# A written-out instruction order searched anew: weight folding ahead of attention, behind a run of matmuls on zeros

## The chip, the cores and the metric

The kernel runs on one core of a Trainium2 chip. The metric is the device time of one execution in microseconds; below are seven runs of the kernel before the change and one profiled execution. The profile splits an execution into a span (first to last instruction of the program) and what lies around it.

## The reference, cut to what matters

Linear attention with the feature map ELU+1, followed by a feed-forward block whose hidden layer is a product of two projections and has no other nonlinearity:

```python
phi = lambda x: np.where(x > 0, x, np.exp(x) - 1.0) + 1.0
kv  = einsum('bhsd,bhse->bhde', phi(k), v);  z = phi(k).sum(axis=2)
att = einsum('bhsd,bhde->bhse', phi(q), kv) / (einsum('bhsd,bhd->bhs', phi(q), z)[..., None] + 1e-6)
x   = att, heads side by side                   # (4608, 512)
out = ((x @ w1) * (x @ w2)) @ w3 @ w_out        # (4608, 512)
```

There are 8 batches of 8 heads, 576 positions and head width 64. The arrays are float32: q, k, v of 9.4 MB each, w1 and w2 512x1024, w3 1024x1024, w_out 1024x512.

## The kernel before, in words

**Fold.** Nothing stands between w3 and w_out, so the kernel multiplies them once into `wf_sb` (1024x512, bf16). Row block i of w3 is loaded with a cast to bf16 (`load_w3`, step E), transposed on TensorE in eight 128x128 pieces (`w3_tr`, step w, L454), copied out of PSUM (L455), and multiplied with w_out in eight matmuls (`wf_mm`, L464; step W for all eight, or U for the first four and W for the last four), then copied to `wf_sb` (L467). Steps C load the two halves of w_out.

**Attention.** Per batch, `load_qkv` brings k (step L), q (M) and v (N): parts 0 and 1 are heads 0-3 and 4-7 of positions 0-511, part 2 is both, part 3 the last 64 positions, as two small DMAs. The feature map takes three passes: exp on ScalarE (steps x for k, X for q, L137), minimum with 1 (y, Y, L141) and max(x+1, e) on VectorE (z, Z, L162). v is cast to bf16 with a column of ones (step v, L171/L176). Step K makes k'v (L199, added at L204), T transposes phi(q) by a DMA (L242), A makes the quotient (L265, L271 to L275), and its transpose into `xt` is step P (TensorE, L285) or D (a DMA, L296). Batch 0 goes another way: phi(q) is transposed on TensorE (steps a and, for the copy out, b; L309, L311), c makes k'v, d masks it (L320), e makes numerator and denominator already transposed (L330), f forms the reciprocal on ScalarE as exp(-ln) (L335, L336), g multiplies (L339).

**Feed-forward.** The 4608 tokens are nine chunks of 512. F c.f does eight matmuls of 128x128 by 128x512 (L371), one ScalarE copy (L376) and one VectorE product (L377); there are eight F per chunk, and each pair of them reads one quarter of w1 and w2, loaded by step B (two DMAs with a cast). Steps h and i are F0.0 and F0.1, interleaved. O c.m makes one output tile from eight matmuls against `wf_sb` (L390) and copies it (L393); S stores it. Q is the last tile.

**What sets the order.** The kernel is scheduled by hand: `ORDER` is a list of steps, and each engine executes its own instructions in exactly this order. A `+` behind a step chooses the other engine: VectorE instead of ScalarE for a copy, GpSimd's DMA queue instead of SyncE's for a load. `GATES` delays four loads until a named load has landed. Three resources tie steps together. Raw q, k, v and w3 share a rotation of five buffers (pool `ld`; the small parts have eight, pool `ldr`), so a load waits until the buffer's last reader is done: the sixth tile waits for the first one's. PSUM has four `mm` banks, taken in turn by F, O, U/W, P and the first two e, and two double banks `at`, taken by w, a, c, e, K and A. And each queue's DMAs carry eight semaphores in rotation, so a DMA is not issued before the one eight places ahead of it on that queue has landed.

Of the kernel before, what the change touches and what calls it, by code (L numbers as in the profile page):

```python
# [18 lines left out]
def kernel(  # L19
# [59 lines left out]
    vt = wpool.tile([P, NJ, H, D + 1], BF16)  # L79
    vr = wpool.tile([P, H // 2, D + 1], BF16)  # L80

    def constants(part):
        if part == 0:
            make_identity(nc, ident)
        elif part == 1:

# [4 lines left out]
            nc.gpsimd.memset(vt[:, :, :, D:D + 1], 1.0)
            nc.gpsimd.memset(vr[:, :, D:D + 1], 1.0)
        else:
            nc.vector.memset(zero, 0.0)  # L94

# [372 lines left out]


    ORDER = """  # L470
    L0.3 M0.0+ X0.0 L0.0+ I1 Y0.0 x0.2 y0.2 M0.1+ Z0.0 x0.0 Z0.1 y0.0 I2 z0.0 z0.4 L0.1+ N0.3+
    x0.1 H12 N0.0+ N0.1+ X0.1 L1.3+ E0 Y0.1 v0.0 L1.2+ v0.1 z0.1 y0.1 B0 v0.2+ I0 Z0.2 z0.2 Z0.3
    E1 C0 x1.2 a0.0 B1 b0.0 C1 c0.0 M1.3+ z0.3 d0.0 e0.0 a0.1 e0.1 f0.0 f0.1 B2 E2 c0.1 y1.2 E3
    b0.1+ M1.2+ w0 d0.1 g0.0 e0.2 e0.3 f0.2 g0.1 B3 h0.0 f0.3 E4 x1.0 g0.2 z1.4 h0.1 h0.2 g0.3
    h0.3 i0.0 y1.0 i0.1 x1.1 w1 z1.0 F0.2 X1.2 z1.1 N1.3+ y1.1 F0.3 U0 z1.2 W0+ F0.4 E5 M2.3+
    F0.5 Y1.2 X1.0 w2+ E6 Y1.0 Z1.0 N1.0+ w3 W1 W2+ X1.1 F0.6 U3 Z1.1 E7 N1.1+ Y1.1 w4 M2.2+
    Z1.2 W3 v1.0+ a1.0 Z1.3 b1.0 w5 F0.7 X2.2 Y2.2 Z1.4 z1.3 w6 W4 w7 L2.2+ a1.1 v1.1+ b1.1 W5+
    v1.2 K1.0+ L3.3+ K1.1+ L2.3+ W6 X2.0 X2.1 A1.0 Y2.0 Z2.0 x2.0 W7 N2.3+ x2.1 x2.2 A1.1 T1.1
    P1.1 O0.0 O0.1 Y2.1 Z2.4 N2.2+ P1.0 L3.2+ y2.2 y2.0 Z2.1 M0.3+ O0.3 z2.0 y2.1 v2.1 P1.2 Z2.2
    P1.3+ v2.0 z2.1 z2.2 X0.2 Z2.3 Y0.2 z2.4 v2.2+ A1.2 x3.0 T2.0 z2.3 O0.2 M3.3+ S0.3 F1.0 x3.2  # L480
    M3.2+ F1.1 X3.0 Y3.0 K2.0+ y3.0 K2.1+ N3.3 X3.1 F1.2 S0.1 M4.3 F1.3 Z0.4 z3.0 x3.1 y3.2 N3.2
    z3.4 X3.2 F1.4 A2.0 Y3.1 F1.5 M4.2+ T0.1 F1.6 A2.1 P2.1 L4.3 v3.2+ F1.7 Z3.0 Y3.2 D1.1 Z3.1
    S0.0 Z3.2 O1.0 y3.1 P2.2+ X4.2 L4.2 z3.1 r0 Z3.3 v3.1 O1.1+ N4.3 v3.0+ P2.0 X4.0 z3.2 O1.3
    F2.0 T2.1 N5.3 z3.3 T3.0 N4.2+ Z3.4 K3.0+ X4.1 A2.2 Y4.0 Y4.2 F2.1 P2.3 K3.1+ Z4.0 x4.0 y4.0
    F2.2 M5.3 Y4.1 O1.2 z4.0 Z4.4 A3.0 F2.3 L6.3 Z4.1 L5.3 x4.2 Z4.2 F2.4 M5.2 x4.1 P3.0+ S0.2
    T3.1 P3.1 z4.1 Z4.3 F2.5 F2.6 A3.1 X5.0 F2.7 v4.2+ v4.0 y4.1 X5.2 L5.2 P3.2 z4.2 X5.1 S1.0
    O2.2+ S1.1 A3.2 y4.2 P3.3+ T4.0 Y5.0 v4.1 z4.3 x5.0 O2.3+ z4.4 F3.0 F3.1 x5.1 K4.0+ K4.1+
    y5.0 Y5.2 z5.0 Z5.4 S1.3 Z5.0 M6.3 x5.2 T4.1 F3.2 F3.3 Z5.1 D3.1 z5.1 O2.1 Y5.1 A4.0 S1.2
    x6.2 L7.3 Z5.2 F3.4 N5.2 F3.5 S2.3 D2.1 L6.2 v5.1 y5.1 A4.1 z5.2 M6.2+ F3.6 D4.0 y6.2 F3.7
    X6.0 S2.2 z5.3 v5.0+ O2.0 S2.1 O3.0 Z5.3 x6.0 x6.1 O3.2 M7.3 y5.2 T5.0 L7.2 z5.4 Y6.0 O3.3  # L490
    v5.2+ y6.0 F4.0 X6.1 X6.2 K5.0+ Y6.2 K5.1+ F4.1 Y6.1 F4.2 z6.0 F4.3 M7.2 Z6.0 N6.2 A5.0 Z6.4
    F4.4 Z6.1 F4.5 A5.1 Z6.2 O3.1 N6.3 F4.6 T5.1 z6.4 F4.7 y6.1 v6.1 S2.0 D5.0 S3.0 v6.2 z6.1
    z6.2 X7.0 O4.0+ Z6.3 Y7.0 x7.0 y7.0 O4.1+ S3.2 x7.2 T6.0 v6.0 O4.3 A4.2 z6.3 K6.0+ D4.1 F5.0
    F5.1 A5.2 X7.1 K6.1+ F5.2 N7.2+ A6.0 T6.1 S3.3 Z7.0 F5.3 X7.2 F5.4 S3.1 D5.1 Y7.1 F5.5 A6.1
    Z7.1 O4.2+ N7.3 y7.2 v7.0 S4.1 A6.2 F5.6 x7.1 F5.7 Z7.2 y7.1 Z7.3 O5.0+ z7.4 Y7.2 S4.0 D6.0
    S4.3 Z7.4 z7.0 S5.0 O5.1 v7.1 z7.1 O5.2+ F6.0 v7.2 z7.2 T7.1 O5.3 z7.3 K7.0+ K7.1+ F6.1 F6.2
    F6.3 T7.0 S4.2 S5.3 A7.0 F6.4 F6.5 A7.1 F6.6 F6.7 S5.1 D7.0 O6.2+ A7.2 O6.3+ O6.0 F7.0 F7.1
    S6.3 D7.1 S5.2 S6.0 F7.2 F7.3 F7.4 O6.1 F7.5 F7.6 F7.7 D6.1 F8.0 F8.1 S6.1 O7.1 S6.2 F8.2
    F8.3 F8.4 F8.5 O7.3 F8.6 F8.7 S7.3 O7.0+ O8.0+ S7.1 O7.2+ S7.0 O8.1 O8.3 S7.2 S8.1 S8.0 S8.3
    Q8.2  # L500
    """
# [129 lines left out]
```

## Time and profile before

| | us |
|---|---|
| median of 7 runs | 256.8 (256.3 to 260.98) |
| the profiled execution, its own time | 257.56 |
| its span | 255.8 |
| TensorE busy in the span | 235.2 |
| VectorE / ScalarE busy | 167.0 / 130.4 |
| start of the matmuls on zeros / of the first useful matmul (a0.0) | 10.53 / 14.99 |
| start of F1.0 (chunk 1), matmuls | 66.66 |

"Busy" is a union of instruction intervals. A TensorE matmul's record is longer than its place in the pipeline: a 128x512 one is listed with 379 ns, but starts 216 ns after the one ahead. "Idle before" is the time in which the engine had nothing, and the name behind the arrow is what ended it. L numbers are lines of the kernel. Issue and landing times of single DMAs are the trace's events; the page gives medians.

### The profile page before, as it was taken

How to read it: one execution, taken by the hardware profiler on the slowest of the kernel's cores; microseconds unless marked ns; L12 is line 12 of the kernel's file. 1: busy time of each engine (PE TensorE's matmuls, PEld its weight loads, DVE VectorE, ACT ScalarE, POOL GpSimd, SP SyncE). 2: the span in 40 equal slices, each digit the busy share in tenths (PEclk: the TensorE clock that was granted, in tenths of full speed). 3: DMA queues.
4: the chain of work that ended last, by engine and by line, in shares of the span. 5: the costliest groups of instructions: out<-in, count | busy, mean ns of one | idle time of the engine just before them, and what ended most of it. 6: DMA issues, size and time to landing. Idle time of an engine off the chain costs nothing.

```text
span 255.8 us, 4477 instructions
## 1 busy us (share of the span) xinstructions
PE 235.2 (92%) x1641; PEld 114.1 (45%) x1660; DVE 167.0 (65%) x425; ACT 130.4 (51%) x206; POOL 43.1 (17%) x69
## 2 busy tenths in 40 slices
PE   0378999999999999999999999989999999999994
PEld 0144444644454554545445444534454444444442
...
DMA  5999999999999999958968946972470231200225
GB/s 185 363 257 202 211 287 233 320 237 326 271 253 282 269 253 285 272 139 273 325 167 212 367 100 164 259 205 25 143 215 3 55 111 62 82 0 0 83 85 164
DMA packets 58726, 49.52 MB, mean 194 GB/s; under 512 B 34448, under 2 KB 49040, under 8 KB 58704
## 3 DMA queue, kind: packets, MB, share of 16 engines
...
## 4 chain that ended last, share of the span: by engine, by line
PE 74%; DMA 17%; POOL 3%; DVE 3%; issue 1%; ACT 1%; ACTq 0%; SPq 0%; DVEq 0%; POOLq 0%
PE b_ps L371 22%; PE a_ps L371 22%; PE o_ps L390 19%; DMA w_sb<-in_moe_w_dram 4%; PE wf_ps L464 4%; DMA qt<-qj 4%; DMA w3b<-in_moe_w_dram 3%; DMA q32r<-in_q_dram 3%; PE kvp L199 3%; DMA k<-in_k_dram 3%; PE nd L265 2%; PE w3p L454 1%; POOL k L120 1%; PE xtp L285 1%; PE o_ps L417 1%
## 5 line engine op out<-in xcount | busy, mean ns | idle before, releaser
L371 PEld LDWEIGHTS <-w_sb 128*128 128x128 bf16 x576 | 54.4, 98 | 66.5 <-DMA w_sb<-in_moe_w_dram 2.5
L377 DVE TENSOR_TENSOR ab<-a_sb,b_ps 128x512 bf16<-128x512 f32 x72 | 49.2, 685 | 50.9 <-PE b_ps L371 46.5
L371 PE MATMUL b_ps<-xt,w_sb 128*128 128x512 bf16 x288 | 74.9, 379 | 1.1 <-DMA w_sb<-in_moe_w_dram 0.6
L371 PE MATMUL a_ps<-xt,w_sb 128*128 128x512 bf16 x288 | 75.1, 380 | 0.2 <-DMA w_sb<-in_moe_w_dram 0.2
L376 ACT COPY a_sb<-a_ps 128x512 f32<-128x512 f32 x72 | 42.1, 586 | 58.6 <-PE a_ps L371 58.6
L390 PE MATMUL o_ps<-wf_sb,ab 128*128 128x512 bf16 x266 | 63.2, 379 | 1.2 <-ACT wf_sb L467 0.4
L390 PEld LDWEIGHTS <-ab 128*128 128x128 bf16 x280 | 26.8, 98 | 31.5 <-issue 0.7
L393 ACT COPY o_sb<-o_ps 128x512 f32<-128x512 f32 x22 | 12.8, 584 | 38.5 <-PE o_ps L390 38.4
L162 DVE SCALAR_TENSOR_TENSOR qj<-q,e 128x256 bf16<-128x256 f32 x64 | 23.8, 417 | 0.1
L162 DVE SCALAR_TENSOR_TENSOR kj<-k,e 128x256 bf16<-128x256 f32 x64 | 23.7, 415 | 0.0
L141 DVE TENSOR_SCALAR e<-e 128x1024 bf16<-128x1024 bf16 x32 | 13.8, 434 | 12.4 <-ACT e L137 12.4
L137 ACT ACTIVATE e<-q 128x1024 bf16<-128x1024 f32 x16 | 16.9, 1061 | 7.1 <-DMA q<-in_q_dram 7.1
L137 ACT ACTIVATE e<-k 128x1024 bf16<-128x1024 f32 x16 | 16.8, 1056 | 2.9 <-DMA k<-in_k_dram 2.2
L275 DVE TENSOR_TENSOR xn<-nd,r 128x512 bf16<-128x512 f32 x28 | 18.0, 686 | 0.0
L120 POOL DMA_DIRECT2D v<-in_v_dram x7 | 5.9, 850 | 66.8 <-ACT vt L171 44.1
L464 PE MATMUL wf_ps<-wo_sb,w3t 128*128 128x512 bf16 x60 | 14.6, 379 | 0.3 <-issue 0.2
L100 PE MATMUL warm<-zero 128*128 128x512 bf16 x12 | 4.6, 565 | 10.5 <-DVE zero L94 10.5
L171 ACT CAST vt<-v 128x1024 bf16<-128x1024 f32 x12 | 12.6, 1048 | 0.3 <-DMA v<-in_v_dram 0.3
L393 DVE COPY o_sb<-o_ps 128x512 f32<-128x512 f32 x13 | 8.9, 686 | 4.4 <-PE o_ps L390 4.4
L120 POOL DMA_DIRECT2D q<-in_q_dram x7 | 6.1, 876 | 33.3 <-ACT a_sb L376 23.6
L464 PEld LDWEIGHTS <-w3t 128*128 128x128 bf16 x64 | 5.9, 98 | 6.3
L199 PE MATMUL kvp<-vt,kj 64*128 64x130 bf16 x224 | 8.7, 217 | 0.0
...
## 6 DMA issues: line engine op xcount, KB each, us to landing
...
```

The lines of the kernel that those rows point to most:

```text
L120: return (nc.gpsimd if alt else nc.sync).dma_start(out=t[:, h0 * W:h1 * W].rearrange("p (h x) -> p h x", x=W), in_=src[b, h0:h1, 0:NJ * P, ...
L137: nc.scalar.activation(out=e, in_=x, func=AF.Exp)
L141: nc.vector.tensor_scalar_min(out=e, in0=e, scalar1=1.0)
L162: nc.vector.scalar_tensor_tensor(out=out, in0=x, scalar=1.0, in1=e, op0=ALU.add, op1=ALU.max)
L199: nc.tensor.matmul(kvp[:, r, i * W:(i + 1) * W], kk[rows], vv[rows], start=(n == 0), stop=(n == (NJ if r == g else NJ - 1)))
L275: nc.vector.tensor_tensor(out=dst.rearrange("p (c u) e -> p u c e", u=2), in0=v4[:, :, :, 0:D], in1=r[0:n].unsqueeze(3).to_broadcast([n, 2 ...
L371: nc.tensor.matmul(ps, w[:, kc, f * P:(f + 1) * P], xt[:, 4 * c:4 * c + 4, kc, :], start=(kc == 0), stop=(kc == KC - 1))
L376: nc.scalar.copy(out=a_sb, in_=a_ps)
L377: nc.vector.tensor_mul(out=abs_[c][:, f, :], in0=a_sb, in1=b_ps)
L390: nc.tensor.matmul(o_ps, ab[:, f, m * P:(m + 1) * P], wf_sb[:, f, :], start=(f == 0), stop=(f == FC - 1))
L393: copy_of(alt)(out=o_sb, in_=o_ps)
L464: nc.tensor.matmul(wfs[i], w3ts[i][:, kc, :], wo_sb[:, kc, :], start=(kc == 0), stop=(kc == FC - 1))
```

## The change

Three things differ. (1) The constants (mask, eps, the columns of ones) are set by VectorE instead of GpSimd. (2) `ORDER` is a new list. It begins with the identity and the constants; TensorE has 44 matmuls on zeros ahead of everything in place of 12, and then the fold (w, U, W of all eight blocks, every W now split) with batch 0's attention threaded between its second half; w3 and w_out are loaded ahead of v, w1 and w2. Loads of batch 3 and later are all on SyncE's queue (six of them were on GpSimd's). Batch 4's phi(q) is transposed on TensorE (a4.0, a4.1, copied by b4.0, b4.1) in place of the DMA T4.0. Many copies change engines. (3) `GATES` names other loads. Everything else, the helper functions and all tile sizes, is as before, and so is each step's arithmetic.

```diff
-            nc.gpsimd.memset(mask, 0.0)
-            nc.gpsimd.memset(mask[0:D, :, 0, :], 1.0)
-            nc.gpsimd.memset(mask[D:P, :, 1, :], 1.0)
-            nc.gpsimd.memset(eps, 1e-6)
-            nc.gpsimd.memset(vt[:, :, :, D:D + 1], 1.0)
-            nc.gpsimd.memset(vr[:, :, D:D + 1], 1.0)
+            nc.vector.memset(mask, 0.0)
+            nc.vector.memset(mask[0:D, :, 0, :], 1.0)
+            nc.vector.memset(mask[D:P, :, 1, :], 1.0)
+            nc.vector.memset(eps, 1e-6)
+            nc.vector.memset(vt[:, :, :, D:D + 1], 1.0)
+            nc.vector.memset(vr[:, :, D:D + 1], 1.0)
...
-    L0.3 M0.0+ X0.0 L0.0+ I1 Y0.0 x0.2 y0.2 M0.1+ Z0.0 x0.0 Z0.1 y0.0 I2 z0.0 z0.4 L0.1+ N0.3+
-    x0.1 H12 N0.0+ N0.1+ X0.1 L1.3+ E0 Y0.1 v0.0 L1.2+ v0.1 z0.1 y0.1 B0 v0.2+ I0 Z0.2 z0.2 Z0.3
-    E1 C0 x1.2 a0.0 B1 b0.0 C1 c0.0 M1.3+ z0.3 d0.0 e0.0 a0.1 e0.1 f0.0 f0.1 B2 E2 c0.1 y1.2 E3
-    b0.1+ M1.2+ w0 d0.1 g0.0 e0.2 e0.3 f0.2 g0.1 B3 h0.0 f0.3 E4 x1.0 g0.2 z1.4 h0.1 h0.2 g0.3
-    h0.3 i0.0 y1.0 i0.1 x1.1 w1 z1.0 F0.2 X1.2 z1.1 N1.3+ y1.1 F0.3 U0 z1.2 W0+ F0.4 E5 M2.3+
-    F0.5 Y1.2 X1.0 w2+ E6 Y1.0 Z1.0 N1.0+ w3 W1 W2+ X1.1 F0.6 U3 Z1.1 E7 N1.1+ Y1.1 w4 M2.2+
-    Z1.2 W3 v1.0+ a1.0 Z1.3 b1.0 w5 F0.7 X2.2 Y2.2 Z1.4 z1.3 w6 W4 w7 L2.2+ a1.1 v1.1+ b1.1 W5+
-    v1.2 K1.0+ L3.3+ K1.1+ L2.3+ W6 X2.0 X2.1 A1.0 Y2.0 Z2.0 x2.0 W7 N2.3+ x2.1 x2.2 A1.1 T1.1
-    P1.1 O0.0 O0.1 Y2.1 Z2.4 N2.2+ P1.0 L3.2+ y2.2 y2.0 Z2.1 M0.3+ O0.3 z2.0 y2.1 v2.1 P1.2 Z2.2
-    P1.3+ v2.0 z2.1 z2.2 X0.2 Z2.3 Y0.2 z2.4 v2.2+ A1.2 x3.0 T2.0 z2.3 O0.2 M3.3+ S0.3 F1.0 x3.2
...
+    I0 I1 L0.3+ L0.0+ x0.2 M0.0+ I2 x0.0 M0.1 y0.0 X0.0 H6 H11 L0.1+ x0.1 N0.3 E0 E1 X0.1 H3 C0
+    C1 H17 E2 Y0.1 H7 Y0.0 E3 w0 w1+ y0.2 L1.3+ U0 y0.1 Z0.0 E4 z0.0 Z0.1 N0.0+ U1 v0.2 W0 w2 W1
+    Z0.2 M1.3+ w3+ z0.4 U2 z0.1 x1.2 W2 w4+ N0.1+ E5 v0.0 U3 W3 a0.0 E6 b0.0 z0.2 c0.0 z0.3 U4
+    X1.2 v0.1+ E7 d0.0 w5+ M1.2+ c0.1 d0.1 Z0.3 e0.0 f0.0 g0.0 W4+ w6 a0.1 b0.1+ U5 y1.2 e0.1
+    w7+ W5+ X1.0 N1.0+ e0.2 X1.1 Y1.0 Z1.0 Y1.1 L2.3+ B0 v1.0 L1.2+ f0.1 Z1.1 U6 B1 W6+ Y1.2
+    f0.2 B2 U7 M0.3+ W7 e0.3 f0.3 g0.1 z1.4 N1.1+ Z1.2 g0.2 B3 h0.0 g0.3 h0.1 h0.2 Z1.3 x1.0
+    h0.3 a1.0 a1.1 y1.0 i0.0 z1.0 i0.1 Z1.4 x1.1 F0.2 y1.1 z1.1 F0.3 X0.2 b1.1 Y0.2 b1.0+ z1.2
+    z1.3 N1.3 F0.4 v1.2 v1.1 F0.5 L2.2+ Z0.4 K1.0+ K1.1+ x2.2 T0.1 F0.6 M2.3+ A1.0 M2.2 F0.7
+    x2.0 O0.3 N2.2 A1.1 y2.0 P1.1 X2.2 x2.1 T1.1 O0.2+ y2.2 P1.2 X2.0 z2.0 z2.1 N2.3 Y2.0 P1.3+
+    X2.1 z2.4 O0.0+ L3.3 Z2.0 P1.0 v2.0 O0.1+ M3.2 v2.2 x3.2 N3.3 y2.1 Z2.1 L3.2 Y2.2 y3.2 Y2.1
+    F1.0 F1.1 Z2.2 Z2.3 F1.2 z2.2 r0 F1.3 z3.4 z2.3 T2.0 M3.3 K2.0+ F1.4 K2.1+ x3.0 A1.2 X3.1
...
-    z6.2 X7.0 O4.0+ Z6.3 Y7.0 x7.0 y7.0 O4.1+ S3.2 x7.2 T6.0 v6.0 O4.3 A4.2 z6.3 K6.0+ D4.1 F5.0
-    F5.1 A5.2 X7.1 K6.1+ F5.2 N7.2+ A6.0 T6.1 S3.3 Z7.0 F5.3 X7.2 F5.4 S3.1 D5.1 Y7.1 F5.5 A6.1
...
+    x7.2 z6.4 A4.2 A5.2 D5.0 X7.2 T6.1 y7.0 O4.0+ y7.2 Z6.3 O4.3+ K6.0+ T6.0 X7.1 D4.1 z7.4 S4.1
+    K6.1+ F5.0 Y7.2 Z7.4 x7.1 F5.1 F5.2 S4.2 Y7.0 F5.3 v7.2 A6.0 F5.4 F5.5 N7.2 A6.1 z7.0 F5.6
...
-    GATES = "B0<L0.1 C0<N0.1 E4<N0.1 M1.2<C1"
+    GATES = "B0<L0.0 C0<L0.0 E4<M0.1 M1.2<E3"
```

More of the change, by code (lines that the diff above doesn't have):

```diff
@@ L477 @@
-    Z1.2 W3 v1.0+ a1.0 Z1.3 b1.0 w5 F0.7 X2.2 Y2.2 Z1.4 z1.3 w6 W4 w7 L2.2+ a1.1 v1.1+ b1.1 W5+
-    v1.2 K1.0+ L3.3+ K1.1+ L2.3+ W6 X2.0 X2.1 A1.0 Y2.0 Z2.0 x2.0 W7 N2.3+ x2.1 x2.2 A1.1 T1.1
-    P1.1 O0.0 O0.1 Y2.1 Z2.4 N2.2+ P1.0 L3.2+ y2.2 y2.0 Z2.1 M0.3+ O0.3 z2.0 y2.1 v2.1 P1.2 Z2.2
-    P1.3+ v2.0 z2.1 z2.2 X0.2 Z2.3 Y0.2 z2.4 v2.2+ A1.2 x3.0 T2.0 z2.3 O0.2 M3.3+ S0.3 F1.0 x3.2
-    M3.2+ F1.1 X3.0 Y3.0 K2.0+ y3.0 K2.1+ N3.3 X3.1 F1.2 S0.1 M4.3 F1.3 Z0.4 z3.0 x3.1 y3.2 N3.2
-    z3.4 X3.2 F1.4 A2.0 Y3.1 F1.5 M4.2+ T0.1 F1.6 A2.1 P2.1 L4.3 v3.2+ F1.7 Z3.0 Y3.2 D1.1 Z3.1
@@ L483 @@
[L483 to L492, printed above, removed]
-    z6.2 X7.0 O4.0+ Z6.3 Y7.0 x7.0 y7.0 O4.1+ S3.2 x7.2 T6.0 v6.0 O4.3 A4.2 z6.3 K6.0+ D4.1 F5.0
-    F5.1 A5.2 X7.1 K6.1+ F5.2 N7.2+ A6.0 T6.1 S3.3 Z7.0 F5.3 X7.2 F5.4 S3.1 D5.1 Y7.1 F5.5 A6.1
@@ L495 @@
[L495 to L500, printed above, removed]
+    I0 I1 L0.3+ L0.0+ x0.2 M0.0+ I2 x0.0 M0.1 y0.0 X0.0 H6 H11 L0.1+ x0.1 N0.3 E0 E1 X0.1 H3 C0
@@ new lines @@
+    z1.3 N1.3 F0.4 v1.2 v1.1 F0.5 L2.2+ Z0.4 K1.0+ K1.1+ x2.2 T0.1 F0.6 M2.3+ A1.0 M2.2 F0.7
+    x2.0 O0.3 N2.2 A1.1 y2.0 P1.1 X2.2 x2.1 T1.1 O0.2+ y2.2 P1.2 X2.0 z2.0 z2.1 N2.3 Y2.0 P1.3+
+    X2.1 z2.4 O0.0+ L3.3 Z2.0 P1.0 v2.0 O0.1+ M3.2 v2.2 x3.2 N3.3 y2.1 Z2.1 L3.2 Y2.2 y3.2 Y2.1
+    F1.0 F1.1 Z2.2 Z2.3 F1.2 z2.2 v2.1 M4.3 r0 F1.3 X3.0 z3.4 z2.3 T2.0 M3.3 K2.0+ F1.4 K2.1+
+    x3.0 A1.2 X3.1 Z2.4 F1.5 Y3.1 N3.2 X3.2 A2.0 X4.2 L4.3 F1.6 F1.7 v3.2 Y3.2 S0.3 A2.1 S0.2
+    y3.0 x3.1 P2.1 Y3.0 y3.1 Z3.4 O1.1 P2.0 x4.2 Y4.2 O1.0 P2.2 v3.1 S0.0 D1.1 O1.2 Z3.0 L4.2
@@ new lines @@
+    z3.0 Z3.1 Z3.2 v3.0 Z3.3 T2.1 z3.1 F2.0 z3.2 M4.2 z3.3 T3.0 x4.0 F2.1 F2.2 K3.0+ y4.0 y4.2
+    A2.2 X4.0 F2.3 K3.1+ S1.0 Y4.0 F2.4 A3.0 z4.0 P2.3 x4.1 Z4.0 z4.1 y4.1 Z4.1 D2.1 N4.2 S0.1
+    M5.2 O1.3 N4.3 F2.5 P3.0 X4.1 A3.1 F2.6 F2.7 Y4.1 P3.1 v4.0 N6.3 X5.0 L5.3 a4.0 b4.0 z4.4
+    L5.2 S1.1 P3.3+ P3.2+ Z4.2 z4.2 Z4.4 O2.1 z4.3 N5.3 Z4.3 v4.2+ M5.3 F3.0 x5.2 Y5.0 v4.1+
+    F3.1 F3.2 a4.1 x5.0 F3.3 x5.1 T3.1 Z5.0 y5.0 S1.3 Z5.1 N5.2 b4.1 O2.0+ y5.2 M6.2 A3.2 F3.4
+    X5.1 K4.0+ S1.2 K4.1+ L6.3 O2.2 M6.3 X5.2 z5.0 D3.1 L6.2 S2.1 A4.0 F3.5 A4.1 Y5.2 v5.1 F3.6
@@ new lines @@
+    z5.1 v5.0 y5.1 z5.4 F3.7 X6.2 Y5.1 z5.2 Y6.2 O3.3+ X6.0 O2.3 D4.0 S2.2 S2.3 Z5.2 Z5.3 x6.0
+    Z6.4 v5.2+ T5.0 z5.3 X6.1 O3.2 F4.0 y6.0 x6.1 K5.0+ K5.1+ S3.3 F4.1 F4.2 Z5.4 Y6.1 S2.0 y6.1
+    Y6.0 z6.0 A5.0 F4.3 F4.4 Z6.0 O3.0 F4.5 N6.2 v6.2+ T4.1 A5.1 F4.6 x6.2 M7.2 z6.1 N7.3 F4.7
+    M7.3 v6.0+ O3.1 v6.1+ S3.0 z6.2 T5.1 L7.2 z6.3 y6.2 L7.3 S3.2 Z6.1 O4.1 Z6.2 x7.0 O4.2 X7.0
+    x7.2 z6.4 A4.2 A5.2 D5.0 X7.2 T6.1 y7.0 O4.0+ y7.2 Z6.3 O4.3+ K6.0+ T6.0 X7.1 D4.1 z7.4 S4.1
+    K6.1+ F5.0 Y7.2 Z7.4 x7.1 F5.1 F5.2 S4.2 Y7.0 F5.3 v7.2 A6.0 F5.4 F5.5 N7.2 A6.1 z7.0 F5.6
@@ L501 @@
+    T7.1 S3.1 F5.7 Z7.0 v7.0 z7.1 y7.1 S4.0 O5.2 Y7.1 D6.0 v7.1 z7.2 O5.3 Z7.1 z7.3 O5.1+ D5.1
+    S5.3 K7.0+ K7.1+ S4.3 S5.1 O5.0 Z7.2 Z7.3 F6.0 F6.1 A6.2 T7.0 A7.2 F6.2 F6.3 S5.2 D7.1 S5.0
+    A7.0 F6.4 F6.5 D6.1 A7.1 F6.6 F6.7 D7.0 O6.2+ O6.1+ O6.0 S6.0 S6.2 O6.3 F7.0 F7.1 F7.2 F7.3
+    F7.4 F7.5 F7.6 F7.7 O7.2 O7.3+ F8.0 F8.1 F8.2 S6.1 S7.2 F8.3 O7.1 F8.4 F8.5 F8.6 F8.7 O7.0+
+    S7.3 S6.3 S7.0 O8.1+ O8.0 S8.1 S8.0 S7.1 O8.3 S8.3 Q8.2
     """
-    GATES = "B0<L0.1 C0<N0.1 E4<N0.1 M1.2<C1"
+    GATES = "B0<L0.0 C0<L0.0 E4<M0.1 M1.2<E3"
```

## The prediction, made before the result was known

> **What bounds the kernel now.** I read the page first, then TensorE by stages, its waits, and the timeline where it waits.
>
> ```profile
> PE 235.2 (92%) x1641; PEld 114.1 (45%) x1660; DVE 167.0 (65%) x425; ACT 130.4 (51%) x206; POOL 43.1 (17%) x69
> ...
> DMA  5999999999999999958968946972470231200225
> ```
>
> TensorE is busy 92%, and the DMA engines are full for the first 90 us: early on the kernel is fed as fast as it computes. By stages (columns: stretch, its length, busy time and count of PE, PEld, DVE, ACT, POOL, clock, DMA share, GB/s):
>
> ```profile
> 0.00:10.00 10.00, 0.00 (x0) 0.00 (x0) 2.35 (x7) 3.70 (x4) 8.66 (x21) 1.00 0.72 249
> 10.00:20.00 10.00, 7.94 (x49) 3.93 (x50) 7.31 (x22) 6.67 (x9) 7.73 (x12) 1.00 1.10 281
> ...
> 70.00:100.00 30.00, 29.84 (x264) 14.99 (x265) 27.57 (x78) 18.92 (x34) 1.14 (x1) 1.00 1.13 265
> ```
>
> After 20 us hardly a gap is left, and from 70 to 100 VectorE is nearly as full (27.57 of 30). What can be won lies in the first 20 us and in TensorE's few waits:
>
> ```profile
> PE warm L100 <- DVE zero L94: 10.5, 1, 10.5
> PE den L330 <- DVE kvz L320: 1.5, 1, 1.5
> PE nd L265 <- DMA qt<-qj: 1.2, 1, 1.2
> ```
>
> The third is A6.0. Its transpose T6.0 was issued late and met a load of v from GpSimd's queue:
>
> ```profile
> 158.85 1.34 SPq L242 DMA_TRANSPOSE qt<-qj  x1
> 159.33 0.88 POOL L120 DMA_DIRECT2D v<-in_v_dram  x1 [44.14 <-ACT vt L171]
> ...
> 168.67 0.42 PE L265 MATMUL nd<-kv,qt 64*128 64x65 bf16 x16 [1.22 <-DMA qt<-qj]
> ```
>
> By the trace's landings T6.0 took 9.8 us; a lone one at 135.2 took 3.8.
>
> **The Trainium skill.** "TensorE: Matmul & The Clock Gate", What's actually happening: the array runs at half clock until about 3.4 us of activity have passed. The trace agrees: of the 12 matmuls on zeros from 10.53 the first nine start 0.427 us apart, and from 14.99 all run at full rate (0.216). "DMA: Bandwidth & Descriptors", Queues, rings and completion order: a DMA engine takes turns between queues, packet by packet; T6.0 beside the v load agrees. No price is taken from a page.
>
> **Part 1: the start.** TensorE's zeros wait for VectorE. ScalarE's first work starts at 0.75; I let VectorE start there too. The memsets cost GpSimd 1.2 us (2.89 to 4.09); VectorE has no such row but zero's (0.27), so 0.5 to 1.2, taken as 0.8: zeros ready at 1.9. On VectorE they cost nothing else, since it had no work until 7.65; without that cover they would cost 0.8. Then 9 x 0.427 + 35 x 0.216 = 11.4: TensorE is free for w0 at 13.3. If the clock never opened, 44 x 0.427 ends at 20.7.
>
> **Part 2: supply.** Landings follow each other by size: half a k, q or v (512 KB) 1.4 us, a w3 block 1.2, half of w_out 2.5, half a B 1.34, 1 MB of q or k 2.6 to 3.3, a small piece 0.2. That is 2.83 us per MiB of float32 (14.9 MiB by 44.9, from 2.9). GpSimd's identity (0.86) comes first, so its DMAs begin near 1.7 to 2.1, 0.6 later; M0.1 goes out on SyncE at 0.74 and fills that time. L0.0 lands about 8.3 (5.2 from issue, as now), which opens C0's gate; M0.0 9.8, L0.1 11.2, E0 12.3, E1 13.5, C0 16.0, C1 18.5, E2 19.7, E3 20.9, E4 22.5, N0.0 24, N0.1 25.4, E5 26.7, E6 27.8, E7 28.9. The rotation of eight semaphores does not bind harder than this: E5 waits for E3, E7 for L1.3.
>
> TensorE then runs w0, w1 (0.45 each), U0 at 16.0, U1, W0 at 18.5, and from there with little waiting: w and U/W cost 0.45 + 2 x 0.86 per block. c0.0 is at 25.9, w5 at 27.7, c0.1 at 28.1, e0.3 at 37.8 to 38.2.
>
> **Part 3: the new wait.** M1.2 takes k0's buffer and waits for z0.3 (VectorE, 26.0, after w4's copy). N1.0 takes q0's and waits for Z0.3, behind w5's copy and d0.1 (two of 0.41): 28.1 + 0.69, c0.1 done 28.95, + 0.8 + 0.75 = 30.6. GpSimd stands from 26.7 to 30.6, and behind it are L2.3, all of B and L1.2. DMA runs dry around 33. N1.0 lands at 36; B0, issued 32.5 to 34, at 39.3; then L1.2 42, B1 45, B2 48, N1.1 50, B3 53 (check: 16.9 MiB x 2.83 + 2.9 = 50.7, plus 2 to 3 dry). On ScalarE N1.0 also holds v1.0, which stands before f0.1: 36 + 1.05, f0.1 and f0.2 1.3 each, W7's copy 0.6, f0.3 1.3, g0.3 0.7, h0.3 at 42.2, done 43.1. So TensorE, free at 38.2, needs 4.9 us for h's 3.46.
>
> F0.2 to F0.5 run on B1 and B2 as they land, to 51.3; K1 waits for v1.1 (52.6), F0.6 for B3 (54.3), then A1.0, F0.7, four O (6.9), A1.1 and four P: F1.0 at 65.3, against 66.66. From w0 that is 52.0 us for about 46.1 of matmuls, by the trace's intervals, and 5.9 of waits. The gain is 1.4: the earlier start, less what the fold waits for bytes.
>
> **Part 4: from F1.0 on.** Batch 4's transposes on TensorE cost 16 x 0.056 = 0.9 and two ScalarE copies (2.0, beside its idle half); A1.2 (0.2 to 0.3) now comes after F1.0: +1.1. T6.0 is issued after O4.0's copy and Z6.3 as before, but A6.0 stands two F later, some 9 us on, and N7.2 is behind T6.0 on the same queue: the stall goes, -1.4 (1.38 by start intervals). Six loads moved to SyncE cost it 0.3 to 0.6 us each to issue; what they wait for now holds back stores and transposes behind them. M2.2 is behind T0.1, which waits for Z0.4 (53.7): issued at 55 instead of 44.95, first read by X2.0 near 61, so hidden; with no cover it would hold ScalarE a few us. T2.0 follows Z2.3 near 72, A2.0 needs it at 77.3: 5 us, enough for a lone transpose, not for a crowded one. VectorE is busy 61.5 of the 70.7 us from F1.0 to F4.0, and up to 28.3 of 30 from 85 to 115; the new list gives it 0.8 more there (counted by steps), so an earlier F1.0 finds VectorE no lighter. Bounds for the new stalls: 0 to 4; I take 0 beyond the old ones.
>
> Sum against the profiled execution: -1.4 + 1.1 - 1.4 = -1.7, span 255.8 to 254.1, its own time 257.56 to 255.9. The median stands 0.76 below the profiled execution's time: **255.1**.
>
> The copies that change engines (four more w3t and some O on VectorE at 0.69, fewer v) add about 2 us to VectorE's 167 and take 2 from ScalarE's 130 over the whole kernel; before F1.0 both engines wait for landings often enough to hide it. The tail keeps its form (after the last F four O in place of five, then Q in two stored halves); nothing taken for it.
>
> **Rivals.**
> - *B comes late* (slower). Place: GpSimd standing at N1.0. Against it: a slack of about a microsecond at h0.0. For it: every B is due within a microsecond of its use, and a 1 MB load from an almost empty queue took 9.3 us (issued 49.27, landed 58.58), not the 7 I use. Each microsecond that B0 lands after 39.3 is a microsecond; at 41 the gain is gone, at 42.5 the kernel is slower by over 0.5%. With L1.2, B1, B2 late too, +4: 259.
> - *Given back* (same). T2.0 or a later transpose stalls A by 1.5, or VectorE binds between F1.0 and F4.0: 256.6. For it: VectorE's 94% between 85 and 115 us, where one late copy passes on; against it: nearly the same work as now.
> - *More than counted* (faster). Supply is one landing ahead, since M0.1, N0.3 and N1.3 go out on SyncE while GpSimd starts; N1.0 and B0 come 1 to 1.5 earlier, and the 0.6 at 69 (69.84, b_ps) goes too: 252.8.
> - *The zeros do not open the clock early*, fold at 20.7 in place of 13.3; W0 waits until 18.5 for C1 anyway and its 4 us of earlier matmuls remain, so +5: 261. The first 12 argue against it.
>
> **Chances and range.** Likeliest case 0.40 (its own range 253.9 to 256.3), more than counted 0.16, given back 0.15, B late 0.26, clock 0.03. 0.5% of 256.8 is 1.3, about what a measurement of this kernel tells from no change: under 255.5 is faster. Of the likeliest case 0.28 goes in, and of the third 0.16: 0.45. Same: 0.11 of the likeliest, most of given back, the edge of B late: 0.25. Slower: 0.30. The range leaves out the clock and the ends of the second and fourth: 252.0 to 259.5.
>
> **What the profile would show.** Right: zeros from about 2, w3p at 13 to 14, a wf_ps wait on wo_sb near 16 and 18; POOL idle for 4 us before a v load near 30, released by VectorE; F0's first matmul at 39 to 41; F1.0 near 65; no wait of nd on qt near 167. Wrong: zeros ending near 20, F1.0 after 67, new waits of nd on qt, of b_ps on w_sb, or ScalarE held by a load with F behind it.

## The result, and the profile after

The changed kernel takes 0.990 of the time of the one before (95% interval 0.9875 to 0.9923): its median is 254.64 us (253.73 to 255.45) beside 257.46 for the runs of the kernel before that were timed with it. The gain is 1.0%. The profiled execution took 254.09 us with a span of 252.0, against 257.56 and 255.8 before. The forecast was 255.1, in a range of 252.0 to 259.5, with 0.45 on faster.

The page of the changed kernel, busy time and the slices of TensorE and the DMA engines:

```profile
PE 242.6 (96%) x1687; PEld 118.5 (47%) x1708; DVE 169.4 (67%) x433; ACT 129.5 (51%) x206; POOL 28.4 (11%) x46
...
PE   6978999999999999999999999999999999999993
...
DMA  5999999959969995988999989379662321030025
```

TensorE's busy time grew by 7.4 us while the span fell by 3.8: the 32 extra matmuls on zeros count as busy and do nothing useful. So the share of 96% is no measure of the gain. What TensorE waited for, all of it that reaches 0.2 us (columns: total, times, longest):

```profile
PE warm L100 <- DVE zero L94: 2.1, 1, 2.1
PE wf_ps L464 <- DMA wo_sb<-in_moe_w_out_dram: 2.0, 2, 1.2
PE o_ps L390 <- issue: 0.3, 2, 0.2
PE w3p L454 <- DMA w3b<-in_moe_w_dram: 0.2, 1, 0.2
```

The waits of den, nd and b_ps are gone, and after 21 us no wait for another engine or a landing has taken their place (what ended the two of o_ps, 0.16 each, the profile doesn't show). The same, by stages cut at F1.0's start (columns as in the prediction):

```profile
0.00:20.00 20.00, 15.84 (x70) 7.01 (x72) 5.93 (x21) 7.13 (x8) 11.58 (x23) 1.00 0.96 224
20.00:63.91 43.91, 43.43 (x339) 23.28 (x342) 35.54 (x87) 32.30 (x49) 16.80 (x24) 1.00 1.11 272
63.91:252.00 188.09, 183.30 (x1282) 88.26 (x1295) 127.90 (x326) 90.09 (x150) 0.00 (x0) 1.00 0.66 173
```

Before, cut in the same way:

```profile
20.00:66.66 46.66, 44.29 (x334) 23.02 (x342) 31.28 (x78) 32.90 (x50) 22.92 (x33) 1.00 1.12 261
66.66:255.80 189.14, 182.96 (x1261) 87.17 (x1271) 126.03 (x320) 87.10 (x145) 3.79 (x4) 1.00 0.65 169
```

F1.0 starts 2.75 us earlier, and from there to the end it is 1.05 us shorter (0.34 more busy, 1.39 less idle). Together that is the 3.8 of the span. The first 2.75 can be split roughly: the first useful matmul starts 0.54 earlier (14.45 against 14.99); A1.2, some 0.3, now stands behind F1.0; and the remaining 1.9 is fewer waits in the fold and batch 0. It can be read as well: these are the waits of before ahead of F1.0, besides den's 1.5 (the b_ps wait for o_sb is left out, it stands behind F1.0).

```profile
PE b_ps L371 <- DMA w_sb<-in_moe_w_dram: 0.6, 2, 0.3
PE o_ps L390 <- ACT wf_sb L467: 0.4, 1, 0.4
...
PE nd L330 <- ACT w3t L455: 0.4, 1, 0.4
PE nd L330 <- DVE kvn L320: 0.3, 1, 0.3
PE a_ps L371 <- DMA w_sb<-in_moe_w_dram: 0.2, 1, 0.2
```

A wait costs some 0.16 us more than its idle time (a matmul's record is that much longer than its place, 0.379 against 0.216). With that, these seven come to 4.6 us, and the three of the changed kernel, two for w_out and one for a w3 block, to 2.75: 1.9 less.

How the start went, in TensorE's timeline (start, length, instruction, idle before it and what ended it):

```profile
2.06 12.55 PE L100 MATMUL warm<-zero 128*128 128x512 bf16 x44 [2.06 <-DVE zero L94]
14.45 1.06 PE L454 MATMUL w3p<-ident,w3b 128*128 128x128 bf16 x16
16.35 1.89 PE L464 MATMUL wf_ps<-wo_sb,w3t 128*128 128x512 bf16 x7 [0.85 <-DMA wo_sb<-in_moe_w_out_dram]
19.43 1.02 PE L464 MATMUL wf_ps<-wo_sb,w3t 128*128 128x512 bf16 x4 [1.20 <-DMA wo_sb<-in_moe_w_out_dram]
```

U0 waits for the first half of w_out (C0, landed 16.22) and W0 for the second (C1, 19.39): those two landings pace the fold. The next place to look at is GpSimd's queue, in its timeline:

```profile
23.98 0.91 POOL L120 DMA_DIRECT2D q<-in_q_dram  x1 [0.23 <-issue]
27.41 0.77 POOL L120 DMA_DIRECT2D v<-in_v_dram  x1 [2.52 <-ACT wf_sb L467]
28.17 1.24 POOL L111 DMA_DIRECT2D k32r<-in_k_dram  x2
29.40 1.52 POOL L431 DMA_DIRECT2D w_sb<-in_moe_w_dram  x2
```

The first line is M1.2, the second N1.0, the fourth B0. GpSimd stands for 2.5 us ahead of N1.0, with B behind it. And A6.0, in SyncE's and TensorE's timelines:

```profile
160.81 1.62 SPq L242 DMA_TRANSPOSE qt<-qj  x1
...
165.69 0.42 SPq L120 DMA_DIRECT2D v<-in_v_dram  x1
...
168.60 0.42 PE L265 MATMUL nd<-kv,qt 64*128 64x65 bf16 x16
```

T6.0 landed at 164.54, 3.74 us after its issue (9.8 before). The v load N7.2 is behind it on the same queue and was issued at 165.69, when T6.0 had landed; A6.0 runs at 168.60 with no wait.

### The profile page after: what moved, and what is told of

Same layout as the page of the kernel before. It is cut to its first block, busy times and chain, and to the rows that moved or that the text cites. A ratio compares the mean times of both kernels' runs of the same rounds, so it can differ in the third digit from the quotient of the medians.

```text
span 252.0 us, 4557 instructions
## 1 busy us (share of the span) xinstructions
PE 242.6 (96%) x1687; PEld 118.5 (47%) x1708; DVE 169.4 (67%) x433; ACT 129.5 (51%) x206; POOL 28.4 (11%) x46
## 3 DMA queue, kind: packets, MB, share of 16 engines
q0 software_dynamic: 8640, 12.85, 21.2%
## 4 chain that ended last, share of the span: by engine, by line
PE 90%; DMA 6%; POOL 1%; issue 1%; ACT 0%; POOLq 0%
PE a_ps L371 26%; PE b_ps L371 25%; PE o_ps L390 24%; PE wf_ps L464 4%; DMA w3b<-in_moe_w_dram 4%; PE kvp L199 3%; PE nd L265 3%; DMA k<-in_k_dram 2%; PE xtp L285 1%; PE w3p L454 1%; PE tp L309 1%; PE o_ps L417 1%; POOL wo_sb L437 1%; POOL k32r L111 1%; PE kvp L219 0%
## 5 line engine op out<-in xcount | busy, mean ns | idle before, releaser
L390 PE MATMUL o_ps<-wf_sb,ab 128*128 128x512 bf16 x263 | 62.3, 379 | 1.1 <-issue 0.3
L141 DVE TENSOR_SCALAR e<-e 128x1024 bf16<-128x1024 bf16 x32 | 13.0, 423 | 10.9 <-ACT e L137 10.9
L100 PE MATMUL warm<-zero 128*128 128x512 bf16 x44 | 12.6, 458 | 2.1 <-DVE zero L94 2.1
L203 ACT COPY kvf<-kvp 128x260 f32<-128x260 f32 x14 | 5.2, 375 | 8.3 <-PE kvp L199 8.2
L100 PEld LDWEIGHTS <-zero 128*128 128x128 bf16 x44 | 4.9, 114 | 9.2 <-issue 3.8
L199 PEld LDWEIGHTS <-kj 64*128 64x128 bf16 x224 | 7.1, 94 | 3.8 <-issue 3.0
```

What stands on the lines that cost most here:

```text
L100: nc.tensor.matmul(ps, zero[:, 0:P], zero, start=True, stop=True)
L141: nc.vector.tensor_scalar_min(out=e, in0=e, scalar1=1.0)
L199: nc.tensor.matmul(kvp[:, r, i * W:(i + 1) * W], kk[rows], vv[rows], start=(n == 0), stop=(n == (NJ if r == g else NJ - 1)))
L390: nc.tensor.matmul(o_ps, ab[:, f, m * P:(m + 1) * P], wf_sb[:, f, :], start=(f == 0), stop=(f == FC - 1))
```

## The experiments

All ratios are to the kernel before, so the changed kernel stands at 0.990 among them. A ratio of an experiment to the changed kernel is the quotient of the two.

### Each half of the new order alone

The lists were joined at F2.0, the first place at which both have done nearly the same; the few steps that one list has done there and the other hasn't were put just before it.

```diff
 # front_new: the new list to F2.0, then the old one
+... T2.1 z3.1  S0.1 M4.2+ N4.3 X4.0 z3.2 O1.3  F2.0 N5.3 z3.3 T3.0 N4.2+ ...
 # back_new: the old list, GATES and constants to F2.0, then the new list
+... z3.2 O1.3  S0.2 Z3.4 x4.2 Y4.2 O1.2 T2.1  F2.0 z3.3 T3.0 ...
```

> The changed order up to F2.0, then the old order from F2.0 on (steps already done left out, the six that are missing put in just before F2.0). Theory 1 (the front is worth 2.8 us, the rest 1.0): F1.0 at 63.9, the waits of the old back half are back (A6.0 near 164 waits about 1.2 for its transpose), span near 253.0, ratio to before 0.989 to 0.992. Rival (the two halves were fitted to each other, the front's gain is given back where VectorE is full): F1.0 at 63.9, but span 255 or more, ratio over 0.996.

> The old order up to F2.0, then the changed order from F2.0 on. Theory 1: F1.0 stays at 66.7, no wait of nd on its transpose near 170, and the 0.9 us of batch 4's transposes on TensorE are paid: span 254.8 to 255.3, ratio 0.995 to 0.999. Rival (the loads on SyncE's queue alone and the new back half carry the gain): span near 253, ratio under 0.993.

front_new: 0.998 (0.9956 to 1.0012), span 255.4. Its F1.0 is at 64.03, as in the changed kernel, but from there to the end it takes 191.4, more than either parent (189.1 and 188.1). Its waits, and the place in the timelines of SyncE, GpSimd and TensorE:

```profile
PE nd L265 <- DMA qt<-qj: 1.9, 2, 1.5
```

```profile
87.95 4.67 SPq L242 DMA_TRANSPOSE qt<-qj  x1
...
88.44 0.89 POOL L120 DMA_DIRECT2D v<-in_v_dram  x1 [13.82 <-DVE qj L162]
...
97.26 0.42 PE L265 MATMUL nd<-kv,qt 64*128 64x65 bf16 x16 [1.47 <-DMA qt<-qj]
```

T3.0 (the first line) met a 1 MB load of v that GpSimd issued half a microsecond later, and took 9.3 us to land. A3.0 stood for it. This is A6.0's stall of the kernel before, in a new place, and A6.0's own is there too (T6.0 8.95 us beside a v load, 0.55 lost). Meeting the load is not the whole cause: in the kernel before T3.0 meets the same load just as closely and lands in 6.1 us, with an issue of 1.65 us on SyncE in place of the 4.67 here. Why is not shown. What the front had won was given back behind it; of the 3.3 us by which this rest is longer than the changed kernel's, the waits of nd are 1.9, some 0.6 are short waits right after A3.0, and the others are not worked out.

back_new: 1.004 (1.0004 to 1.0077). I had expected 0.995 to 0.999, and that was wrong. In its profiled execution (256.24 us, the fastest of its runs, where their median is 258.3) F1.0 is at 65.51, from F1.0 to the end it takes 189.0, and no matmul of nd waits for a transpose. So the stall was gone there and the time was not. What its other runs waited for isn't seen in that profile and stays open.

Neither half alone gains: -0.2% and +0.4%, where both together give -1.0%. The two parts of the sum don't add. An order written out by hand fits the times at which its own earlier part delivers.

### The stall at A6.0

```diff
 # old_a6_later: the old order, A6.0 moved behind F5.3
-... F5.2 N7.2+ A6.0 T6.1 S3.3 Z7.0 F5.3 X7.2 ...
+... F5.2 N7.2+ T6.1 S3.3 Z7.0 F5.3 A6.0 X7.2 ...
```

> The kernel before with A6.0 moved behind F5.3, one F (1.73 us) later, nothing else. Theory (the 1.4 us at A6.0 is only a transpose that is asked for too late for its place): the wait of nd on qt near 167 is gone or under 0.2, T6.0 still takes 9 to 10 us beside the v load, time from F1.0 to the end 187.6 to 188.0 in place of 189.1, ratio to before 0.994 to 0.997. Rival (the time comes back, since VectorE's quotient and the transposes behind it, A6.1 and D6.0, come later): from F1.0 to the end 188.8 or more.

0.997 (0.9944 to 0.9999), span 253.6. The transpose is as slow as before (issued 157.97, landed 167.60), and its reader doesn't mind:

```profile
168.23 0.42 PE L265 MATMUL nd<-kv,qt 64*128 64x65 bf16 x16
```

From F1.0 to the end this kernel takes 187.5, against 189.1 before and 188.1 in the changed one. From F5.0 to F6.0, the stretch with the stall, it is 23.03 in place of 24.31: the stall was worth 1.28. The other 0.3 lies ahead of F2.0, where the wait at 69 is absent; that isn't this edit's doing. So with one step moved the old rest is no slower than the new one, and in the old order the move of A6.0 is enough.

In the changed kernel it was not what helped. A6.0 stands one F later there, but other work went ahead of T6.0: from T6.0's issue to A6.0 are 7.8 us (160.81 to 168.60), and before the change it was 8.6 (158.85 to 167.45, when TensorE was ready for it). A transpose of 9.8 us would have held A6.0 by 2.0 (an estimate from these figures). What helped is that T6.0 met no load and took 3.7. For the queue, the next two runs.

```diff
 # six_gpsimd: the changed kernel, the six loads on GpSimd again
-M3.2  M3.3  M4.2  N4.2  M6.2  N7.2
+M3.2+ M3.3+ M4.2+ N4.2+ M6.2+ N7.2+
 # old_six_sync: the kernel before, the same six on SyncE, places kept
-M3.3+ M3.2+ M4.2+ N4.2+ M6.2+ N7.2+
+M3.3  M3.2  M4.2  N4.2  M6.2  N7.2
```

> The changed kernel with the six loads of batch 3 and later (M3.3, M3.2, M4.2, N4.2, M6.2, N7.2) back on GpSimd's queue, at the same places of the order. Theory 1 (the queue matters only where such a load meets a transpose that TensorE is about to need, and the new order leaves A6.0 two F more): within 0.4 us of the changed kernel. Rival (a second queue takes turns with the transposes, whose latency grows to 7 to 10 us): new waits of nd on qt, 1 to 3 us slower.

> The kernel before with one part of the change alone: the same six loads on SyncE's queue, everything else as before. Theory (a transpose takes 9 to 10 us beside a 1 MB load from the other queue and 4 to 6 without): T6.0 lands by 164, the 1.4 us wait at A6.0 is gone, span 254.0 to 254.6, ratio to before 0.994 to 0.997. Rival (a load that waits for its buffer now stands in SyncE's queue ahead of stores and transposes): a new wait of nd on qt or of a copy on o_sb, ratio 1.000 or more.

six_gpsimd: 0.994 (0.9892 to 0.9985). From F1.0 on it is the changed kernel to a few hundredths:

```profile
65.34:253.40 188.06, 183.30 (x1282) 88.25 (x1295) 128.22 (x327) 90.79 (x150) 4.34 (x4) 1.00 0.62 169
```

188.06 against 188.09. T3.0 takes 7.0 us to land beside the load N4.2, and still comes in time. N7.2 is on the other queue again and doesn't meet T6.0 either: it went out early, at 155.39, and had landed at 162.07, just before T6.0's issue at 162.23; T6.0 took 3.65. So what counts is when the load goes out, and that the six are free of stalls on both queues is in part the luck of these times. The longer span of this kernel is the start's: C1 landed at 20.49 instead of 19.39. The queue of these six loads is worth nothing at the new places that these runs can show.

old_six_sync: 1.034 (1.0254 to 1.0429), the largest difference of all. T6.0 now lands in 5.2 us and A6.0 doesn't wait, as the theory said, but the rival takes over. TensorE's waits, and ScalarE's timeline at the place:

```profile
PE a_ps L371 <- ACT a_sb L376: 6.6, 1, 6.6
```

```profile
80.19 1.06 ACT L137 ACTIVATE e<-q 128x1024 bf16<-128x1024 f32 x1 [7.99 <-DMA q<-in_q_dram]
```

M3.2 stood behind T2.0 and others in SyncE's list, was issued at 71.82 instead of 62.50 and landed at 80.17 instead of 70.52. The exp that reads it (step X, ScalarE) waited 8 us for it, with the copy of an F queued behind. I had looked for the cost in nd or in o_sb; the engine was another. And the wait cost more than itself, as the stretch behind it shows (columns as above; the clock is the last but two):

```profile
82.00:89.00 7.00, 5.73 (x29) 2.06 (x29) 5.61 (x17) 3.57 (x6) 0.00 (x0) 0.51 0.69 222
```

From 82.1 to 88.9 the granted clock was a half, and the matmuls from 83.27 on start 0.427 us apart. F1.0 to F2.0 takes 32.49 in place of 22.75: 6.6 of the 9.7 is the wait, and 2.8 the clock (an estimate: half of the 5.6 us from 83.27 to 88.9). A load's queue can't be chosen apart from its place in that queue.

### The start

```diff
 # const_gpsimd: six constants on GpSimd again
-            nc.vector.memset(mask, 0.0)
+            nc.gpsimd.memset(mask, 0.0)
...
 # no_zeros: no matmuls on zeros
-... X0.0 H6 H11 L0.1+ ... X0.1 H3 C0 C1 H17 E2 Y0.1 H7 Y0.0 ...
+... X0.0 L0.1+ ... X0.1 C0 C1 E2 Y0.1 Y0.0 ...
 # m01_late: M0.1 to GpSimd behind E4, L0.1 behind C1, their readers moved likewise, six zeros fewer,
 # and no gate on E4
-... I2 x0.0 M0.1 y0.0 X0.0 H6 H11 L0.1+ x0.1 N0.3 E0 E1 X0.1 H3 C0 C1 H17 E2 ... Z0.1 N0.0+ ...
+... I2 x0.0 N0.3 y0.0 X0.0 H6 H11 E0 E1 Y0.0 H3 C0 C1 L0.1+ H11 E2 ... Z0.1 M0.1+ N0.0+ ...
 # sync_head: L0.3 to SyncE behind M0.1, no zeros, no gate on C0
-I0 I1 L0.3+ L0.0+ x0.2 M0.0+ I2 x0.0 M0.1 ...
+I0 I1 M0.1 L0.3 L0.0+ x0.2 M0.0+ I2 x0.0 ...
```

no_zeros leaves out the 44 matmuls on zeros and nothing that is read.

> The changed kernel with the six memsets of the constants back on GpSimd, ahead of its first load. Theory (the front is bound by the bytes of w_out, and they are counted from GpSimd's first issue): GpSimd's loads begin 1.2 later (2.7 in place of 1.46), C0 and C1 land 0.8 to 1.2 later, F1.0 0.8 to 1.2 later, ratio to the changed kernel 1.003 to 1.005. Rival (M0.1, N0.3 and N1.3 from SyncE fill the time): F1.0 within 0.3.

> The changed kernel without any of the 44 matmuls on zeros. Theory (they only open the clock; the fold starts when w3 and w_out land): w0 at 12.6, U0 still at 16.4, but at half clock: U0 and U1 take 3.4 in place of 1.7, W0 at 19.9 to 20.3, and the first 3.4 to 7 us of steady work from 16.4 run slow: F1.0 1 to 3 us later, ratio to the changed kernel 1.004 to 1.012. Rival (TensorE waits for bytes until 20.6 anyway, and the clock opens meanwhile): F1.0 within 0.4. Second rival (the clock falls back between bursts and stays low to about 30): 4 us or more.

> The changed kernel with M0.1 (second half of batch 0's q, first read by a0.1 near 32) taken from the head of SyncE's queue and put on GpSimd's behind E4, and L0.1 behind C1; the feature map's steps that read them move behind. Six fewer zeros, and the gate of E4 left out. Theory (the front is bound by bytes, in the order in which they are asked for): E0 to C1 land 1.3 to 2.6 earlier, C0 at 13.6 to 14.0, C1 at 16.8 to 17.2, w2 at 19.4; F0 starts 0.4 to 1.0 earlier, F1.0 at 63.0 to 63.6, ratio to the changed kernel 0.996 to 0.999. Rival (v, E5 and B land when they did, and TensorE waits for them instead): F1.0 unchanged.

> The changed kernel with two small loads (L0.3) moved from the head of GpSimd's queue to SyncE's, behind M0.1, so that GpSimd's first large load goes out 1.35 earlier; without zeros, and without the gate of C0. Theory (the front is bound by when w_out's bytes are asked for): L0.0 lands near 7.4, C0 at 14.9 to 15.4, C1 at 18.1 to 18.6, F0 starts 0.6 to 1.2 earlier than 39.2, F1.0 at 62.8 to 63.4, ratio to the changed kernel 0.995 to 0.998. Rival (the DMA engines are already full from 2 us on, and the same bytes land in another order): C1 and F1.0 within 0.3.

const_gpsimd: 0.9935 (0.991 to 0.996). The memsets hold GpSimd's first load until 2.24 instead of 1.46; C1 lands at 20.11 instead of 19.39 and F1.0 starts at 64.94 instead of 63.91. That fits the 0.8, but one profile doesn't show it: C1 landed as late in other kernels with the head unchanged (20.14 in t4_dma, 20.49 in six_gpsimd). The ratio is 0.35% over the changed kernel's, and the intervals still overlap. The clock is a rival: in this execution it was a half from 18.3 to 21.7, over matmuls of the fold, and in 16 of this kernel's 20 runs the mean granted clock was 0.993 or less, in the changed kernel's never under 0.997. On VectorE the six take about 0.9 us in a time in which it has nothing to do.

no_zeros: 0.991 (0.9889 to 0.994), span 251.9, F1.0 at 63.77. TensorE's timeline:

```profile
12.23 1.03 PE L454 MATMUL w3p<-ident,w3b 128*128 128x128 bf16 x8 [12.23 <-DMA w3b<-in_moe_w_dram]
...
15.97 4.43 PE L464 MATMUL wf_ps<-wo_sb,w3t 128*128 128x512 bf16 x12 [1.50 <-DMA wo_sb<-in_moe_w_out_dram]
```

Twelve of the fold's own matmuls take 4.43 us from 15.97, eight of them at half clock, and all the while W0 could not have begun: C1 landed at 19.27. The waiting time paid for the opening of the clock. The run of zeros, the change's most visible part, buys nothing that these runs can show.

m01_late: 0.998 (0.9952 to 1.0008), slower than the changed kernel. E0 and E1 land 1.6 us earlier, but C0 doesn't: its gate waits for L0.0. C1 lands at 18.79, and then the postponed 1 MB stands in front of everything else: E5 lands 2.3 us later, w3p waits 1.5 us, N1.0 is issued at 31.34, and F1.0 starts at 66.99. Not all of it is the bytes: from the end of the w3p wait on the granted clock was a half (21.2 to 24.6), which is worth up to 1.6 us of the 3.0 by which F0 is late (an estimate: half of the 3.2 from w3p's start). What SyncE fetched while GpSimd was starting had been free, or nearly.

sync_head: 0.994 (0.9914 to 0.9972). C1 was asked for four microseconds earlier (5.63 instead of 9.57) and landed at 19.59 instead of 19.39. F1.0 is at 64.67, not earlier than in the changed kernel. The theory fell, and the rival stands: with the DMA engines full (their share was 0.96 over the first 20 us of the changed kernel), asking earlier for the same bytes in the same order did not land them earlier. That the bytes ahead of a block and the moment of the first one set its landing fits these runs; it is not shown by itself.

### The wait ahead of N1.0

```diff
 # n10_late: N1.0 waits for E7's landing
-    GATES = "B0<L0.0 C0<L0.0 E4<M0.1 M1.2<E3"
+    GATES = "B0<L0.0 C0<L0.0 E4<M0.1 M1.2<E3 N1.0<E7"
```

> The changed kernel with one more gate: N1.0 (first half of batch 1's v) waits until E7 has landed, so it is issued near 31.0 in place of 27.4, about where the prediction put it, and L2.3, B and L1.2 behind it. Theory (the stand of GpSimd at N1.0 is what was mis-sized, and it sits on the path): B0 lands 1.5 to 2 later (39.5), h ends near 43.3 in place of 42.7, F1.0 at 64.9 to 65.3 in place of 63.9, ratio to the changed kernel 1.003 to 1.006. Rival (slack of supply takes it): F1.0 within 0.3 of 63.9, ratio within 0.001.

0.996 (0.9936 to 0.9984), 0.6% over the changed kernel. GpSimd's timeline, and TensorE's waits:

```profile
31.83 0.77 POOL L120 DMA_DIRECT2D v<-in_v_dram  x1 [6.42 <-ACT lr L335]
```

```profile
PE a_ps L371 <- ACT a_sb L376: 1.0, 1, 1.0
PE b_ps L371 <- DMA w_sb<-in_moe_w_dram: 0.3, 1, 0.3
```

and ScalarE's timeline ahead of the first wait:

```profile
44.12 1.06 ACT L137 ACTIVATE e<-k 128x1024 bf16<-128x1024 f32 x1 [2.62 <-DMA k<-in_k_dram]
45.08 1.06 ACT L376 COPY a_sb<-a_ps 128x512 f32<-128x512 f32 x2
```

N1.0 is issued 4.4 us later than in the changed kernel, B0 lands at 40.34 instead of 37.73, and F1.0 starts at 66.25, 2.34 later (about 0.5 of it is C1, which landed later in this execution). That is more than was expected (64.9 to 65.3). F's b_ps waits for B, as the prediction's slower rival said. The larger wait is F held by ScalarE, and ScalarE is held not by N1.0's copy, which the prediction had named, but by the exp that reads L1.2, the load behind B0: it landed at 44.09 instead of 40.30. In the changed kernel B0 had 1.7 us to spare (landed 37.73, first needed at 39.39), L1.2 only 0.4 (landed 40.30, its exp at 40.69). So 1.8 us is the price of the whole queue coming later, and the tight load is L1.2.

### Batch 4's transposes

```diff
 # t4_dma: the DMA T4.0 in place of the transposes on TensorE; "both": t4_dma and sync_head together
-... L5.3 a4.0 b4.0 z4.4 ... Z4.3 v4.2+ ... F3.2 a4.1 x5.0 ... N5.2 b4.1 O2.0+ ...
+... L5.3 z4.4 ... Z4.3 T4.0 v4.2+ ... F3.2 x5.0 ... N5.2 O2.0+ ...
```

> The changed kernel with T4.0 (one DMA transpose on SyncE, placed behind Z4.3) in place of a4.0, a4.1, b4.0, b4.1. Theory (the transposes on TensorE cost 16 x 0.056 = 0.9 and nothing waits for a DMA that has 9 us to land): 0.9 us less from F3.0 on, ratio to the changed kernel 0.996 to 0.998. Rival (SyncE's queue is full there, T4.0 lands late or holds a load back): a wait of nd on qt near 119 or of ScalarE on a load, ratio 1.000 or more.

> sync_head and t4_dma together. Theory: the two add up, 1.5 to 2 us below the changed kernel, ratio to it 0.992 to 0.995. Rival: as for either of them.

t4_dma: 1.000 (0.9959 to 1.0045), 1% over the changed kernel. TensorE's busy time from F1.0 falls by 0.53 (183.30 to 182.77), and a wait of 1.9 comes in, from F1.0 to the end 189.6 in place of 188.1. Its timelines of SyncE and TensorE:

```profile
112.13 2.23 SPq L242 DMA_TRANSPOSE qt<-qj  x1
...
127.29 0.53 SPq L120 DMA_DIRECT2D k<-in_k_dram  x1
...
128.99 5.06 SPq L296 DMA_TRANSPOSE xt<-xn  x1
```

```profile
136.61 1.02 PE L371 MATMUL a_ps<-xt,w_sb 128*128 128x512 bf16 x4 [1.92 <-DMA xt<-xn]
```

T4.0 (112.13) landed in 4.3 us. It was not late itself, but SyncE stood 0.9 us ahead of it and then issued it for 2.2 us, and what is behind it shifted: the 1 MB load of k at 127.29 was issued at 121.17 in the changed kernel, so 6.1 later where F1.0 is only 1.5 later. The transpose behind that load landed at 136.48 instead of 132.20, and F4.0 waited for it. The half microsecond that batch 4's transposes cost TensorE buys SyncE's queue free.

both: 1.001 (0.9976 to 1.0037), with the same wait (1.6) at F4.0. It shows nothing further.

No kernel here is faster than the changed one. One was not tried: the new front with the old rest and A6.0 moved. front_new says that T3.0 would still meet its load there. Not separated either are the copies that change engines and the new gates.

## Why the prediction came out as it did

The direction, the place and the order of size were right: faster, most of it ahead of F1.0, the rest from A6.0. The reasons given for both parts were wrong in one step each (parts 3 and 4). The span was put at 254.1 and is 252.0. Of that difference 1.4 lies ahead of F1.0 (65.3 predicted, 63.91 measured) and 0.7 behind it.

**Part 1, the start.** Zeros ready at 1.9, measured 2.06. TensorE was to be free for w0 at 13.3 and was at 14.45: fourteen matmuls ran at half clock, not nine. It cost little, since E1 landed at 13.70. The clock rival fell. That the part didn't matter at all, the prediction didn't see; no_zeros showed it.

**Part 2, supply.** The landings were placed one by one at 2.83 us per MiB: E0 12.3 (12.46), C0 16.0 (16.22), C1 18.5 (19.39), E4 22.5 (23.41), E7 28.9 (30.72). They hold within 0.2 us until C0 and drift to 1.8 at E7. The largest mis-sized term is the second half of w_out, 2.5 in the sum and 3.2 in the trace; from E4 to E7 it is 7.3 in place of 6.4.

**Part 3, the new wait, is the step that failed.** "M1.2 takes k0's buffer and waits for z0.3", "N1.0 takes q0's and waits for Z0.3": the five buffers don't pass on in strict turn, as I had taken it and as the description of the kernel says. M1.2 was issued at 23.98, some 3 us before z0.3 was done (26.84), so it can't have waited for it. The semaphores say what did: M1.2 waits for TensorE (a w3 block's buffer, free after step w3), and N1.0 for VectorE, a wait that ends at 26.88, with z0.3, so for what M1.2 was said to wait for. (The bracket in GpSimd's timeline names ScalarE's copy only because its semaphore came last, at 27.14.) So GpSimd stood 2.5 us instead of 3.9, N1.0 was issued at 27.41 instead of 30.6, and B0 landed at 37.73 instead of 39.3, B1 at 43.0 instead of 45, B2 at 45.6 instead of 48, B3 at 49.9 instead of 53. F0's first matmul came at 39.18 all the same (39.3 predicted), since the fold was late by about the drift of part 2; behind it the waits that were priced didn't come. From w0 to F1.0 I had 5.9 us of waits and the trace leaves 3.4 (49.46 less the same 46.1 of matmuls). Against the sum the start is 1.15 late and the waits are 2.5 fewer; that the second error is the larger is luck.

**Part 4.** The stall at A6.0 was -1.4, and idle time from F1.0 fell by 1.39. The match is partly chance: the idle time gone is A6.0's 1.2 and 0.4 at 69, less 0.3 of new short gaps. The added work was +1.1 and is 0.34 in TensorE's busy time; t4_dma gives 0.53 for batch 4's share, where the sum had 0.9. Of the two causes named for the end of the stall, "A6.0 stands two F later, some 9 us on" is a misreading: it stands one F later, and 7.8 us after T6.0's issue, which is less than before. The move would have been enough in the old order (old_a6_later) and was not in the new. The other cause, N7.2 behind T6.0, is what the profile shows, with the correction that the time at which N7.2 goes out does it and not the queue (six_gpsimd). The bound of 0 to 4 for new stalls was taken at 0, and 0 was measured. That this was not safe is shown by front_new, old_six_sync and t4_dma, each of which has such a stall.

**The rivals.** "More than counted" describes the profile best: N1.0 and B earlier, the 0.6 at 69 gone. But its reason was wrong: supply wasn't ahead, the buffers were others. "B comes late" did not happen and is real: in n10_late B0 lands 1.0 after 39.3 and F1.0 starts at 66.25, where the price that was given says 66.3. The path is in part another, through L1.2. "Given back" fell in this kernel, where VectorE has 26.21 of the 30 us from 70 to 100, less than before; it is what happened to front_new.

How sure the front's 2.75 is: C1's landing varies between 19.27 and 20.49 over eight kernels whose instructions ahead of it are the same or nearly so, and F1.0 follows it by 44.4 to 45.3 in every one. Four kernels with the old front start F1.0 at 65.51 to 67.34 (mean 66.4), four with the new one at 63.91 to 65.44 (mean 64.7). The mean gain is 1.7, not far from the 1.4 predicted; one pair of profiles shows the lucky end. Behind F1.0 the profiles hardly differ: from F1.0 to F8.0 the changed kernel and six others with its rest (six_gpsimd, no_zeros, const_gpsimd, m01_late, n10_late, sync_head) take 159.93 or 159.94 us, every one. 1.7 at the start and 1.05 behind it make 2.75, which fits the 2.8 between the medians.
